# A gated mix of a state-space convolution and a GEGLU network: shared coefficient tables, a rotated contraction, products under the feed-forward matmuls, and one activation for GELU

## Chip, cores and metric

The kernel runs on one core of a Trainium2 chip. The metric is the device time of that core in microseconds (us), where lower is better. Each kernel was executed several times. Executions come in two states: in the slow one, TensorE's granted clock (the share of its full speed that the chip allowed, as the profile shows it) is lower over the whole run, and the time is longer. The span that a profile shows is the time from the first to the last instruction, and it is about 1.8 us shorter than the device time of the same execution.

## The reference

The output is `g*a + (1-g)*b` for an input of 2048 positions and 640 channels. `a` is a convolution with a generated filter, `b` is a feed-forward network, and `g` is a gate per position.

```python
# a: the filter of channel d at position l is a sum over N = 128 states
l = jnp.arange(L).astype(A_re.dtype)                # bfloat16
P = jnp.exp(logdA[:, :, None] * l[None, None, :])   # logdA = exp(log_dt) * (A_re + i A_im)
K = jnp.einsum("dn,dnl,dn->dl", Cc, P, dB).real     # 640 x 2048, dB = exp(log_dt) * B
# ... y = irfft(rfft(K, padded) * rfft(u, padded)), cut to L ...
a = y + u * Dskip
# b, with F = 1728
b = (gelu(x @ w_gate) * (x @ w_up)) @ w_down        # tanh form of GELU
g = sigmoid((x * gate_w).sum(-1, keepdims=True))    # x = u
```

One detail matters. The positions `l` are cast to bfloat16. They stay exact up to 256, then come in steps of 2 up to 512, of 4 up to 1024 and of 8 up to 2048. So `K` has only 257 + 3*128 = 641 different columns, not 2048.

## The kernel before

It works in strict stages. For each block of 64 channels it forms two tables, of 32 and 64 entries, so that their products give all 2048 positions. TensorE forms the phases, VectorE (DVE) reduces their range, and ScalarE (ACT) evaluates Exp, Abs and Sin. TensorE then contracts the tables over the 128 states:

```python
nc.scalar.activation(out=c1[:], in_=p1[:], func=ACT.Abs)
# ... c2; then Sin of c1, c2, p1, p2 (six ACT passes per block), four multiplications by the exponentials
nc.tensor.matmul(psK[:, ci, :], lhsT=c1[:, dl, :], rhs=c2[:, dl, :], start=True, stop=False)
nc.tensor.matmul(psK[:, ci, :], lhsT=p1[:, dl, :], rhs=p2[:, dl, :], start=False, stop=True)
```

After that come the forward transforms of filter and input (512 matmuls of 320 columns), the products of the two spectra on DVE, and the inverse transform (256 matmuls). Only then are the weights of the feed-forward network loaded. GELU is put together from a sigmoid:

```python
nc.scalar.copy(out=Gs[:fsz], in_=pGt[:fsz])
nc.scalar.copy(out=Us[:fsz], in_=pUt[:fsz])
nc.vector.tensor_tensor(out=q[:fsz], in0=Gs[:fsz], in1=Gs[:fsz], op=ALU.mult)
# ... two more DVE instructions on q ...
nc.scalar.activation(out=sg[:fsz], in_=q[:fsz], func=ACT.Sigmoid, scale=GELU_C)
nc.vector.tensor_tensor(out=sg[:fsz], in0=sg[:fsz], in1=Gs[:fsz], op=ALU.mult)
nc.vector.tensor_tensor(out=HT[:fsz, ft, toks], in0=sg[:fsz], in1=Us[:fsz], op=ALU.mult)
```

The down projection (448 matmuls) and the gated blend end the kernel.

## Time and profile before

The kernel had four executions, with a median of 777.4 us (775.29 to 991.85). The profiled one was the slow one:

```profile
core 0: 990.1 us, clock 0.569
```

The windows view cuts the span at the borders of the stages. The columns are the window, its length, the busy us of PE, PEld (weight loads), DVE, ACT and POOL (instruction counts in brackets), the granted clock, the share of DMA engine time, and GB/s.

```profile
0.00:370.00 370.00, 237.93 (x1690) 108.61 (x1691) 306.97 (x428) 289.26 (x229) 5.76 (x25) 0.61 0.09 18
391.00:505.00 114.00, 113.86 (x475) 62.53 (x475) 41.75 (x51) 41.26 (x61) 0.00 (x0) 0.56 0.00 1
505.00:622.00 117.00, 62.84 (x254) 33.67 (x252) 88.89 (x77) 0.26 (x1) 0.00 (x0) 0.53 0.00 0
622.00:642.00 20.00, 0.00 (x0) 0.00 (x0) 0.78 (x1) 0.00 (x0) 0.00 (x0) 0.51 0.97 243
642.00:861.00 219.00, 218.01 (x641) 76.92 (x642) 105.97 (x278) 95.89 (x170) 0.00 (x0) 0.55 0.06 21
861.00:990.10 129.10, 111.58 (x448) 46.58 (x446) 28.20 (x34) 12.16 (x18) 0.00 (x0) 0.55 0.06 21
```

The limit changes from stage to stage. Coefficients (to 370) are bound by DVE and ACT together, the transforms (to 505) by TensorE, the products (to 622) by DVE. From 622 to 642 TensorE does nothing while a weight load fills the DMA engines. The gate and up projection (to 861) is bound by TensorE, with DVE busy for half of it.

The groups view lists line of the kernel (L478 is line 478), engine, operation, tiles, shapes and count, then busy us and mean ns, then the idle time before them and what ended it.

```profile
L478 PE MATMUL pGt<-xT,Wg 128*128 128x512 bf16 (+1 forms) x280 | 118.5, 582 | 21.1 <-DMA Wg<-in_B_w_gate_dram 21.1
L283 PE MATMUL psK<-c,c 128*32 128x64 bf16 x640 | 68.2, 229 | 14.5 <-DVE c L272 9.3
L257 DVE TENSOR_SCALAR kM<-pph 128x512 f32<-128x512 f32 x120 | 80.6, 684 | 41.8 <-PE pph L248 26.9
```

The first line holds the 21 us weight gap. A "mean ns" of a matmul is its own latency, and matmuls overlap, so their cost is busy time divided by count (here 118.5 us / 280 = 423 ns, at a clock of 0.55).

### The profile page before, as it was taken

What the parts mean: (1) busy time and instruction counts of PE and PEld (TensorE: products, weight loads), DVE (VectorE), ACT (ScalarE), POOL (GpSimd) and SP (SyncE); (2) the same over time, 40 slices, a digit from 0 to 9 for tenths busy, and PEclk for the clock granted to TensorE, in tenths of its full rate; (3) what the DMA queues carried; (4) which work ended last, traced back from release to release, by engine and by line L of the source; (5) the groups of instructions that cost most, each with busy time, mean ns of one, the idle gap of its engine ahead of it and who ended that gap; (6) DMA issues with size and microseconds to landing.
All of it is one profiled execution on the core that took longest, in us unless ns stands there. A gap on an engine that the chain in (4) does not pass through costs nothing.

```text
span 990.1 us, 8897 instructions
## 1 busy us (share of the span) xinstructions
PE 755.7 (76%) x3556; PEld 333.8 (34%) x3556; DVE 585.5 (59%) x906; ACT 452.8 (46%) x492; POOL 6.3 (1%) x26
## 2 busy tenths in 40 slices
PE   0076787777797556999996605199999999988997
PEld 0022233323343253555553302033333333333333
DVE  6969878888888964045737897044544545422222
ACT  1259989899989956333310000044444444301000
POOL 2000000000000000000000000000000000000000
PEclk9975555555555555555555555555555555555555
DMA  2000000000000040000000000840000000000000
GB/s 53 0 0 1 1 12 11 11 1 12 12 12 11 1 129 11 0 1 1 1 1 0 1 0 0 222 153 1 0 1 0 1 0 1 0 21 21 20 27 21
DMA packets 44650, 19.01 MB, mean 19 GB/s; under 512 B 37248, under 2 KB 43328, under 8 KB 44608
## 3 DMA queue, kind: packets, MB, share of 16 engines
q1 hardware_dynamic: 44608, 18.44, 7.2%
q8 instruction: 28, 0.46, 0.2%
q14 instruction: 14, 0.11, 0.0%
HBM read 9.91 MB, written 2.62 MB: 13 GB/s over the span
## 4 chain that ended last, share of the span: by engine, by line
PE 66%; DVE 16%; ACT 14%; SPq 2%; DMA 1%; issue 1%; ACTq 0%; DVEq 0%
PE pU L372 11%; PE pD L502 11%; PE pGt L478 11%; PE pUt L481 11%; PE pY L408 6%; PE pa L252 2%; PE psK L283 2%; PE psK L284 2%; ACT c L267 2%; ACT p L269 2%; DVE kM L257 2%; DVE M L399 2%; DVE t L398 2%; DVE p L258 2%; ACT c L265 1%; DVE M L396 1%
## 5 line engine op out<-in xcount | busy, mean ns | idle before, releaser
L478 PE MATMUL pGt<-xT,Wg 128*128 128x512 bf16 (+1 forms) x280 | 118.5, 582 | 21.1 <-DMA Wg<-in_B_w_gate_dram 21.1
L502 PE MATMUL pD<-Wd,HT 128*128 128x512 bf16 (+1 forms) x448 | 111.8, 423 | 12.3 <-ACT b_sb L505 12.3
L484 ACT CAST Gs<-pGt 128x512 bf16<-128x512 f32 (+1 forms) x56 | 32.8, 586 | 191.4 <-PE pGt L478 191.4
L481 PE MATMUL pUt<-xT,Wu 128*128 128x512 bf16 (+1 forms) x280 | 118.3, 584 | 0.0
L257 DVE TENSOR_SCALAR kM<-pph 128x512 f32<-128x512 f32 x120 | 80.6, 684 | 41.8 <-PE pph L248 26.9
L408 PE MATMUL pY<-M,FI 128*128 128x320 bf16 x256 | 63.5, 443 | 54.1 <-DVE M L399 54.1
L253 PE MATMUL pph<-RX,b_bf 128*128 128x512 bf16 x80 | 40.8, 514 | 53.7 <-DVE p L258 52.7
L283 PE MATMUL psK<-c,c 128*32 128x64 bf16 x640 | 68.2, 229 | 14.5 <-DVE c L272 9.3
L283 PEld LDWEIGHTS <-c 128*32 128x32 bf16 x640 | 55.9, 116 | 66.1 <-DVE K L285 36.7
L258 DVE SCALAR_TENSOR_TENSOR p<-kM,pph 128x512 bf16<-128x512 f32 x120 | 77.8, 676 | 0.2
L488 DVE TENSOR_TENSOR q<-Gs 128x512 bf16<-128x512 bf16 (+1 forms) x56 | 23.8, 425 | 86.8 <-ACT Gs L484 86.8
L502 PEld LDWEIGHTS <-HT 128*128 128x128 bf16 x448 | 46.7, 123 | 78.0 <-issue 74.0
L284 PE MATMUL psK<-p,p 128*32 128x64 bf16 x640 | 67.9, 229 | 3.1 <-DVE p L273 3.1
L509 DVE TENSOR_TENSOR diff<-a_sb,b_sb 128x640 f32<-128x640 bf16 x16 | 13.2, 825 | 96.5 <-ACT b_sb L505 96.5
L372 PE MATMUL pU<-K_sb,FK 128*128 128x320 bf16 x256 | 62.7, 437 | 9.7 <-ACT FK L359 8.3
L478 PEld LDWEIGHTS <-Wg 128*128 128x128 bf16 (+1 forms) x280 | 37.0, 133 | 91.4 <-issue 91.4
L486 ACT CAST Us<-pUt 128x512 bf16<-128x512 f32 (+1 forms) x56 | 32.8, 586 | 66.3 <-PE pUt L481 49.2
L505 ACT CAST b_sb<-pD 128x640 bf16<-128x640 f32 x16 | 11.1, 692 | 112.5 <-PE pD L502 112.5
L408 PEld LDWEIGHTS <-FI 128*128 128x128 bf16 x256 | 34.1, 134 | 83.3 <-DVE M L399 50.5
L372 PE MATMUL pU<-a_sb,FU 128*128 128x320 bf16 x256 | 61.7, 438 | 0.0
L481 PEld LDWEIGHTS <-Wu 128*128 128x128 bf16 (+1 forms) x280 | 37.7, 135 | 69.9 <-issue 69.8
L284 PEld LDWEIGHTS <-p 128*32 128x32 bf16 x640 | 57.0, 118 | 6.2 <-issue 6.2
(140 smaller groups left out, 1120.8 us busy)
## 6 DMA issues: line engine op xcount, KB each, us to landing
K_sb<-K SPq DMA_DIRECT2D x40, 64.0 KB, 2.3
a_sb<-in_A_u_dram SPq DMA_DIRECT2D x4, 640.0 KB, 5.2
out_dram<-o_sb SPq DMA_DIRECT2D x16, 160.0 KB, 1.8
Wg<-in_B_w_gate_dram SPq DMA_DIRECT2D x1, 2160.0 KB, 8.5
Wu<-in_B_w_up_dram SPq DMA_DIRECT2D x1, 2160.0 KB, 13.3
Wd<-in_B_w_down_dram SPq DMA_DIRECT2D x1, 2080.0 KB, 19.2
dsk<-in_A_Dskip_dram SPq DMA_DIRECT2D x1, 160.0 KB, 3.4
Are<-in_A_A_re_dram SPq DMA_DIRECT2D x1, 160.0 KB, 3.5
```

The lines of the kernel that those rows point to most:

```text
L253: nc.tensor.matmul(pph[:], lhsT=lhs_b, rhs=rhs_rx, start=True, stop=True)
L257: nc.vector.tensor_scalar(out=kM[:], in0=tau_src, scalar1=MAGIC, scalar2=None, op0=ALU.add)
L258: nc.vector.scalar_tensor_tensor(out=pt[:, :, xs], in0=kM[:], scalar=-MAGIC, in1=tau_src, op0=ALU.add, op1=ALU.subtract)
L283: nc.tensor.matmul(psK[:, ci, :], lhsT=c1[:, dl, :], rhs=c2[:, dl, :], start=True, stop=False)
L284: nc.tensor.matmul(psK[:, ci, :], lhsT=p1[:, dl, :], rhs=p2[:, dl, :], start=False, stop=True)
L372: nc.tensor.matmul(pU[:, h, 0:DH], lhsT=tab[:, k, q, f0:min(512, f0 + 256):2], rhs=src[:, 4 * b + k, h * DH:(h + 1) * DH], start=(k == 0), ...
L408: nc.tensor.matmul(pY[:, h, 0:DH], lhsT=FI[:, ft, q, 128 * mo:128 * mo + 128], rhs=M[:, q, ft, h * DH:(h + 1) * DH], start=(q == 0 and ft ...
L478: nc.tensor.matmul(pGt[:fsz, :], lhsT=Wg[:, kt, f0:f0 + fsz], rhs=xT[:, kt, toks], start=(kt == 0), stop=(kt == nkt - 1))
L481: nc.tensor.matmul(pUt[:fsz, :], lhsT=Wu[:, kt, f0:f0 + fsz], rhs=xT[:, kt, toks], start=(kt == 0), stop=(kt == nkt - 1))
L484: nc.scalar.copy(out=Gs[:fsz], in_=pGt[:fsz])
L486: nc.scalar.copy(out=Us[:fsz], in_=pUt[:fsz])
L502: nc.tensor.matmul(pD[:, d0:d0 + dn], lhsT=HT[:fsz, ft, toks], rhs=Wd[:fsz, ft, d0:d0 + dn], start=(ft == 0), stop=(ft == nft - 1))
```

## The change

The intent is to do less coefficient work, and to let stages that use different engines run at the same time. The kernel is largely rewritten, with all tiles at fixed places in one memory area, which the profile calls `arena`. Cut to its core and regrouped by purpose:

```diff
 # 1. Coefficients at 32 x 21 = 672 positions, four chunks of 160 channels; the second table holds these bases:
+X2 = [0, 1, 2, 3, 4, 5, 6, 7, 256, 258, 260, 262, 512, 516, 768, 772, 1024, 1280, 1536, 1792, 2048]
 # ... exponentials: one activation per table entry, its step given as the scale; phases are 16-bit
 # fixed-point numbers that wrap by themselves, so Abs and DVE's range reduction go ...
-            nc.scalar.activation(out=c1[:], in_=p1[:], func=ACT.Abs)
-                    nc.tensor.matmul(psK[:, ci, :], lhsT=c1[:, dl, :], rhs=c2[:, dl, :], start=True, stop=False)
-                    nc.tensor.matmul(psK[:, ci, :], lhsT=p1[:, dl, :], rhs=p2[:, dl, :], start=False, stop=True)
+            for g in range(gh):
+                for q in range(2):
+                    for j in range(4):
+                        d = G4 * j + gh * hb + g
+                        nc.tensor.matmul(psK[hb][32 * j:32 * j + 32, NX2 * g:NX2 * g + NX2], lhsT=cs1[:, q, :, d],
+                                         rhs=cs2[:, q, :, d], start=(q == 0), stop=(q == 1))
 # ... the transform table of the filter sums the positions that round to one value ("selection") ...
 # 2. The input's transform runs inside the coefficient stage:
+        phases(k)
+        last_sin[0] = sines(k)
+        u_some(2)
+        scaled(k)
 # 3. Filter transform and products go by frequency tile, and are free to run under the feed-forward matmuls:
+    for ft in range(NF):
+        kb, gt = k_fwd(ft)
+        Mf.append(products(ft, kb, gt))
 # 4. GELU is one activation:
-                nc.scalar.activation(out=sg[:fsz], in_=q[:fsz], func=ACT.Sigmoid, scale=GELU_C)
+                gi = nc.scalar.activation(out=Gs[:], in_=pG[:], func=ACT.Gelu_apprx_tanh)
 # 5. The inverse transform joins the down projection, both at 320 columns, and the gate goes into the last additions:
+                    nc.tensor.matmul(pD[:, 0:DH], lhsT=HT[c][0:fz, ft, ts], rhs=Wd[0:fz, ft, hs],
+                                     start=(ft == 0), stop=(ft == NFT - 1))
 # ...
+                        nc.tensor.matmul(pY[:, 0:DH], lhsT=tab[:, ft, q, ts], rhs=Mf[ft][:, q, c, hs],
+                                         start=(q == 0 and ft == 0), stop=(q == 1 and ft == NF - 1))
 # ... many lines cut ...
```

In the contraction, both operands now step through memory by 160 elements, which is 320 bytes.

## The prediction

> **What bounds the kernel now.** The profiled execution is a slow one: 990 us, mean granted TensorE clock 0.569, against 775 to 778 us for three others. By busy time per stretch: coefficient generation, 0 to 370 us (ACT busy 289, DVE 307); forward transforms to 505 (PE 114 of 114); products and inverse to 622 (DVE 89, PE waits 54 for DVE); 20 us without PE work (waits: 21.1 for the Wg load); gate and up projection to 861 (PE 218 of 219); down projection to the end. The groups show ACT spending 167 us in Abs and Sin and about 55 in table loads.
>
> Here a 512-column matmul starts every 382 ns, a 320-column one every 0.22 us (timeline). The Trainium skill ("TensorE: Matmul & The Clock Gate", Back-to-back issue gap) gives N/2.4 + 2.5 ns warm: 216 and 136 ns. With those (estimate) the PE-bound stages lose about 195 of the 214 us between slow and fast runs, so I take fast runs to be near full clock. No trace here shows one.
>
> **What changes.** The coefficients are evaluated at 672 points instead of 2048, over tables of 32 + 21 entries instead of 32 + 64; +/- pairs share sines. ACT (estimates: 0.83 ns per element, from traced lengths, plus 0.1 to 0.2 us each): 106 Exp 40, 20 Sin 42, tables 8, 32 spectrum copies 20, table loads 10. Total 120 us in place of 290. DVE here: phases and scaling about 22 us per 160-column chunk, four chunks, plus weights, selection tables and copies: 140 in place of 307; DVE becomes the pacer. The input transform (256 matmuls) hides here. The kernel transform falls from 256 to 144 matmuls; coefficient selection adds 44.
>
> GELU becomes one activation: five DVE instructions per FFN tile become one (112 to about 20 us). Products keep their elements but split by frequency: about 114 us of DVE, now under the FFN's 138 us of PE. The inverse (256 matmuls) merges with the down projection (448), all at 320 columns: 704 x 136 ns = 96 us.
>
> **New risk.** The contraction keeps 1280 small matmuls, but reads both operands with a 320-byte stride. Before they were contiguous, about 29 ns apiece. The skill ("SBUF — State Buffer", Door 1: The DMA port swizzle) says each access crossing to a new 16-byte line pays a penalty; no run here shows its size. I take 50 ns: 64 us. The second table has one buffer and DVE's PSUM copies queue in order, so I count most of this as exposed.
>
> **Sum, fast state.** First sine at 53; DVE's 20 groups, second exponentials and exposed contraction about 155, so FFN starts near 207; FFN with products 155 (PE 138; DVE 134, starting late); last stage with its weight load 100; tail 5. About 465 us.
>
> Predicted 465 us, 80% range 410 to 535. Faster by over 2%: 0.98; within: 0.01; slower: 0.01. A slow run would be about 600.
>
> **What shows it right.** Groups: contraction spacing 30 to 100 ns; DVE about 140 us before the FFN; Sin about 42 us. Waits: ACT or DVE on the contraction. Stages: FFN near 155 us with PE busy 85% or more; last stage with PE always busy; the weight gap gone.
>
> **What would make it wrong.** Contraction at 100 ns or more (+65 us) or without penalty (-25); small DVE instructions costing more than 0.25 us start to start; DVE trailing PE at the FFN's end, delaying the inverse; denser PE work being granted a lower clock.

## Result and profile after

The changed kernel took 450.95 us (median of 8 executions, 449.02 to 452.74). By then the kernel before had 13 executions with a median of 777.03 us; only the first one, at 991.85, was slow; no run here explains why. The ratio is 0.5804, with a 95% interval of 0.5794 to 0.5814. Ratios here are the mean time of one kernel's fast runs over that of the other's fast runs of the same rounds, so they are not quite the ratio of the medians quoted. The result is correct.

The profiled execution is a fast one. The cores view, and the windows view with the same columns as before:

```profile
core 0: 448.3 us, clock 0.931
```

```profile
0.00:52.30 52.30, 5.00 (x16) 1.90 (x17) 30.22 (x63) 36.58 (x72) 0.95 (x7) 1.00 0.22 50
52.30:90.00 37.70, 26.45 (x425) 17.79 (x425) 32.37 (x80) 24.45 (x22) 1.74 (x12) 0.86 0.08 22
90.00:130.00 40.00, 29.13 (x432) 16.47 (x431) 32.17 (x64) 35.61 (x68) 0.00 (x0) 0.87 0.18 42
130.00:168.00 38.00, 20.03 (x395) 13.61 (x394) 32.21 (x72) 19.86 (x17) 0.00 (x0) 0.79 0.23 62
168.00:193.50 25.50, 7.74 (x345) 5.99 (x344) 9.25 (x22) 6.02 (x4) 0.00 (x0) 0.57 0.96 215
193.50:345.60 152.10, 146.34 (x758) 69.35 (x759) 138.08 (x194) 84.13 (x141) 0.00 (x0) 0.99 0.13 33
345.60:445.00 99.40, 99.17 (x679) 63.57 (x678) 45.39 (x76) 0.00 (x0) 0.00 (x0) 1.00 0.13 43
```

The coefficient stage, with the whole input transform in it, ends at 193.5 instead of near 390. Over the three middle windows DVE is the busiest engine (96.8 of 115.7 us, against 79.9 for ACT and 75.6 for TensorE). It does not pace the stage alone: from 90 to 130, where the second exponentials run, ACT is busier (35.6 of 40 us), and DVE itself waits 15.0 us for the contraction. From 193.5 to 345.6, TensorE (146 of 152 us) and DVE (138) are both nearly full. That is the overlap at which the change aims. In the last 99.4 us TensorE is always busy.

The groups that answer to those shown of before:

```profile
L490 PE MATMUL pG<-arena 128*128 128x512 bf16 x260 | 67.7, 386 | 1.5 <-DVE arena L505 1.4
L369 PE MATMUL psK<-arena 128*32 128x21 bf16 x1280 | 20.7, 213 | 26.0 <-DVE arena L356 15.5
L339 ACT ACTIVATE arena<-arena 128x2240 bf16<-128x2240 int16 (+1 forms) x20 | 43.4, 2177 | 22.9 <-DVE arena L332 20.6
```

The gate matmuls no longer wait for their own weights. The 1280 small matmuls of the contraction are busy for 20.7 us in all, 16 ns apiece. The sines, with their cosines, take 43.4 us.

The seam between the two halves is not clean. The timeline of TensorE and of SP (SyncE, the engine that issues most transfers) from 178 us on shows start, length, engine, line, what, how many, and in square brackets the idle time before and its releaser:

```profile
178.12 3.66 PE L369 MATMUL psK<-arena 128*32 128x21 bf16 x237 [15.51 <-DVE arena L356]
...
182.94 0.53 SPq L456 DMA_DIRECT2D arena<-in_B_w_up_dram  x1
183.51 5.83 SPq L470 DMA_TRANSPOSE arena<-in_A_u_dram  x2
...
186.04 1.41 PE L369 MATMUL psK<-arena 128*32 128x21 bf16 x83 [4.25 <-issue]
...
189.44 11.82 SPq L376 DMA_DIRECT2D arena<-arena  x16
...
193.53 2.32 PE L493 MATMUL pU<-arena 128*128 128x512 bf16 x5 [3.41 <-DMA arena<-in_B_w_up_dram]
```

TensorE waits 15.5 us for DVE to scale the last tables, pauses for 4.25 us within the contraction (see the run with another loop order below), and waits 3.4 us for the up weights. The 16 small copies that spread the filter's values over partitions (L376) are issued one after another, 0.74 us each, and only from 189.4 on. The first product needs them, and starts at 204.8. From there to 340.9 DVE is busy for 132 of 136 us and TensorE for 133 (windows view). That the late start of the products sets the end of this stage is read from several traces: in seven of them (this one and six of the experiments below) the last product starts 136.3 to 138.2 us after the first filter spectrum is out, whenever that is. This is its end:

```profile
340.42 0.48 DVE L441 TENSOR_TENSOR arena<-arena 128x640 bf16<-128x640 bf16 x1
...
340.93 0.37 SPq L517 DMA_DIRECT2D arena<-in_B_w_down_dram  x1
...
345.61 2.11 PE L536 MATMUL pD<-arena 128*128 128x320 bf16 x12 [1.47 <-DMA arena<-in_B_w_down_dram]
```

The rest of the down weights goes where the products had their buffers. So its load starts only after the last product, and the last stage with it.

### The profile page after: what moved, and what is told of

Its sections match the earlier page's. It is cut to its first block, busy times and chain, and to the rows that moved or that the text cites. A ratio compares the mean times of both kernels' runs of the same rounds, so it can differ in the third digit from the quotient of the medians.

```text
span 448.3 us, 7434 instructions
## 1 busy us (share of the span) xinstructions
PE 333.9 (74%) x3046; PEld 188.7 (42%) x3046; DVE 320.1 (71%) x568; ACT 206.6 (46%) x321; POOL 2.7 (1%) x19
## 4 chain that ended last, share of the span: by engine, by line
PE 43%; DVE 31%; ACT 12%; DMA 6%; SPq 5%; issue 2%; DVEq 0%; ACTq 0%
PE pD L536 14%; PE pY L543 8%; DVE arena L441 5%; PE pT L413 5%; DVE arena L440 4%; PE pT L204 4%; DVE arena L438 3%; PE psK L369 3%; PE pU L493 3%; PE pG L490 3%; DVE arena L498 3%; DVE arena L437 3%; ACT arena L339 3%; SPq L470 2%; SPq L376 2%; DMA arena<-in_B_w_up_dram 2%
## 5 line engine op out<-in xcount | busy, mean ns | idle before, releaser
L204 PE MATMUL pT<-arena 128*128 128x320 bf16 x256 | 51.0, 366 | 72.3 <-ACT arena L174 43.9
L536 PE MATMUL pD<-arena 128*128 128x320 bf16 x448 | 69.7, 300 | 1.5 <-DMA arena<-in_B_w_down_dram 1.5
L493 PE MATMUL pU<-arena 128*128 128x512 bf16 x260 | 67.6, 384 | 3.4 <-DMA arena<-in_B_w_up_dram 3.4
L490 PE MATMUL pG<-arena 128*128 128x512 bf16 x260 | 67.7, 386 | 1.5 <-DVE arena L505 1.4
L204 PEld LDWEIGHTS <-arena 128*128 128x128 bf16 x256 | 29.3, 117 | 93.0 <-ACT arena L174 45.6
L536 PEld LDWEIGHTS <-arena 128*128 128x128 bf16 x448 | 43.6, 97 | 26.1 <-issue 10.1
L339 ACT ACTIVATE arena<-arena 128x2240 bf16<-128x2240 int16 (+1 forms) x20 | 43.4, 2177 | 22.9 <-DVE arena L332 20.6
L495 ACT ACTIVATE arena<-pG 128x512 bf16<-128x512 f32 x52 | 31.1, 598 | 39.9 <-PE pG L490 38.3
L496 ACT CAST arena<-pU 128x512 bf16<-128x512 f32 x52 | 30.5, 587 | 27.1 <-PE pU L493 27.0
L543 PE MATMUL pY<-arena 128*128 128x320 bf16 x256 | 40.5, 300 | 2.2 <-DVE arena L505 2.2
L538 DVE SCALAR_TENSOR_TENSOR arena<-pD,omg,arena 128x320 f32<-128x320 f32 x32 | 17.6, 550 | 34.0 <-PE pD L536 34.0
L369 PE MATMUL psK<-arena 128*32 128x21 bf16 x1280 | 20.7, 213 | 26.0 <-DVE arena L356 15.5
L493 PEld LDWEIGHTS <-arena 128*128 128x128 bf16 x260 | 25.0, 98 | 33.0 <-DMA arena<-in_B_w_up_dram 4.2
L490 PEld LDWEIGHTS <-arena 128*128 128x128 bf16 x260 | 25.4, 99 | 31.9 <-issue 4.4
L440 DVE TENSOR_TENSOR arena<-arena 128x2560 bf16<-128x2560 bf16 (+3 forms) x32 | 31.4, 982 | 2.5 <-ACT arena L415 2.5
L545 DVE SCALAR_TENSOR_TENSOR arena<-pY,g_f,arena 128x320 bf16<-128x320 f32 x32 | 17.6, 552 | 19.8 <-PE pY L543 19.8
L441 DVE TENSOR_TENSOR arena<-arena 128x2560 bf16<-128x2560 bf16 (+3 forms) x32 | 31.4, 982 | 0.0
L543 PEld LDWEIGHTS <-arena 128*128 128x128 bf16 x256 | 22.5, 98 | 14.4 <-issue 2.4
## 6 DMA issues: line engine op xcount, KB each, us to landing
arena<-in_B_w_up_dram SPq DMA_DIRECT2D x1, 2160.0 KB, 10.5
```

Source lines behind the costliest of these rows:

```text
L204: nc.tensor.matmul(pU[:, h, 0:DH], lhsT=tab[:, k, q, fsl(ft)], rhs=ublk[b][:, k, h * DH:(h + 1) * DH], start=(k == 0), stop=(k == 3))
L339: return nc.scalar.activation(out=dst, in_=ph_tile(k)[:].bitcast(I16)[:, :, 0:n, 0:2 * CH:2], func=ACT.Sin, scale=SIN_SCALE)
L369: nc.tensor.matmul(psK[hb][32 * j:32 * j + 32, NX2 * g:NX2 * g + NX2], lhsT=cs1[:, q, :, d], rhs=cs2[:, q, :, d], start=(q == 0), stop=(q ...
L440: nc.vector.tensor_tensor(out=t1[:, 0:nb, :], in0=U[:, 1, 0:nb, :], in1=g[k1], op=ALU.mult)
L441: nc.vector.tensor_tensor(out=dst, in0=dst, in1=t1[:, 0:nb, :], op=op1)
L490: nc.tensor.matmul(pG[:], lhsT=Wg[:, kt, f0:f0 + 128], rhs=xT[:, kt, :], start=(kt == 0), stop=(kt == NKT - 1))
```

## Experiments

Twelve kernels were run. The runs of the kernel before had medians of 777.14, 776.18 and 775.81 us. The changed kernel itself was timed apart from these, so a difference from it is also a difference of two ratios.

My theory was this. The gain has two sources of about equal rank: less coefficient work on ACT and DVE, and DVE's products moved under TensorE's feed-forward work, which only fits because the new GELU frees DVE. The rivals were: the slow profile had misled me about fast runs; the new GELU is worth something by itself; the contraction's cost is off the critical path; and the memory stride makes the contraction slow, or else the rotation over column groups makes it fast.

### The kernel before, once more, for a fast profile

There is no edit.

> The kernel before, unchanged, to get a profile of its fast state, which no trace so far shows. Theory of the prediction (fast means near full clock, so that the PE-bound stages shrink and the coefficient stage hardly does): 777 us, granted clock above 0.85; gate and up projection 120 to 130 us, last stage 70 to 80, forward transforms 68 to 75, coefficient stage 335 to 360. Rival (fast runs are throttled less, but still throttled): clock 0.7 to 0.8, gate and up projection 145 to 165 us, and the coefficient stage below 320.

It took 775.31 us at a clock of 0.854. Its time is that of the fast ones. Its windows, cut at its own stage borders:

```profile
0.00:359.00 359.00, 189.30 (x1700) 89.65 (x1700) 309.51 (x445) 288.74 (x230) 6.32 (x26) 0.81 0.09 19
359.00:437.00 78.00, 73.21 (x511) 50.52 (x512) 45.51 (x68) 54.74 (x75) 0.00 (x0) 0.95 0.00 1
437.00:537.00 100.00, 42.19 (x259) 27.07 (x257) 93.01 (x83) 0.69 (x1) 0.00 (x0) 0.71 0.00 0
537.00:558.00 21.00, 0.00 (x0) 0.00 (x0) 0.55 (x1) 0.00 (x0) 0.00 (x0) 0.60 1.02 269
558.00:687.50 129.50, 126.79 (x640) 57.44 (x640) 99.65 (x270) 89.23 (x167) 0.00 (x0) 0.99 0.08 29
687.50:769.00 81.50, 68.45 (x449) 34.78 (x448) 29.40 (x41) 13.24 (x21) 0.00 (x0) 1.00 0.09 31
```

The stages that TensorE bounds shrink from 219 to 129.5 us (gate and up) and from 129 to 81.5 us (down). The coefficient stage, bound by DVE and ACT, goes only from 370 to 359. This is what the prediction had worked out from the slow profile. Its size was somewhat too large: the transforms, the gate and up projection and the last stage lost 36, 89.5 and 43 us, 169 in all, where the estimate for the stages bound by TensorE was about 195.

It also gives the account of the gain, with spans. Before, coefficients and input transform took 359 + 35 = 394 us (the 256 input matmuls are one stretch of 34.9 us in this trace) and the rest 379.5 us. After, these are 193.5 and 254.8 us. So about 200 us come from the coefficient side and about 125 us from everything behind it. No run takes back one of the coefficient edits alone, so how the 200 us divide is not shown. Candidates are the fewer table entries per channel (53 instead of 96), the range reduction that DVE no longer does (L257 and its partner L258 filled 158 us of the slow profile), the Abs passes, and the input transform that now runs alongside.

### GELU as one activation, in the kernel before

```diff
-                nc.scalar.copy(out=Gs[:fsz], in_=pGt[:fsz])
+                nc.scalar.activation(out=Gs[:fsz], in_=pGt[:fsz], func=ACT.Gelu_apprx_tanh)
 # ... the chain of q and sg is gone ...
-                nc.vector.tensor_tensor(out=HT[:fsz, ft, toks], in0=sg[:fsz], in1=Us[:fsz], op=ALU.mult)
+                nc.vector.tensor_tensor(out=HT[:fsz, ft, toks], in0=Gs[:fsz], in1=Us[:fsz], op=ALU.mult)
```

> One part of the change alone: the kernel before with the GELU as a single activation, four DVE instructions and a sigmoid per tile fewer. Theory: in the kernel before the gate and up projection is bound by PE (2.16 us of matmuls per tile against about 1.65 us of DVE), so removing 80 to 90 us of DVE work buys nothing: 765 to 780 us, within 2%. Rival: in the fast state DVE and ACT pace that stage: 740 to 755 us.

It took 771.67 us (770.89 to 772.41), a ratio of 0.9928 (0.9913 to 0.9943). Its window of the gate and up stage:

```profile
557.60:683.20 125.60, 125.42 (x641) 57.52 (x641) 23.37 (x55) 69.17 (x116) 0.00 (x0) 0.98 0.09 32
```

DVE's work in the gate and up stage fell from 99.7 to 23.4 us, yet the stage only went from 129.5 to 125.6 us, with TensorE busy for 125.4. Here DVE was not what the stage waited for.

### The sigmoid chain put back into the changed kernel

```diff
-                gi = nc.scalar.activation(out=Gs[:], in_=pG[:], func=ACT.Gelu_apprx_tanh)
+                nc.scalar.copy(out=Gs[:], in_=pG[:])
-                    nc.vector.tensor_tensor(out=ht[:, ft, :], in0=Gs[:], in1=Us[:], op=ALU.mult)
+                    gelu_chain(ht[:, ft, :], Gs[:])
+                    nc.vector.tensor_tensor(out=ht[:, ft, :], in0=ht[:, ft, :], in1=Us[:], op=ALU.mult)
```

> The same part undone in the changed kernel: the sigmoid chain back, everything else as changed. Theory: there the DVE shares the stage with the products (138 us busy of 152), so the chain's four extra instructions per tile, about 1.25 us x 56 = 70 us, land on the critical path: stage 210 to 225 us instead of 152, total 505 to 530 us. Rival (PE still bounds the stage, as in the kernel before): 451 to 460 us.

It took 521.51 us, a ratio of 0.6716 (0.6701 to 0.6731), 70.6 us more than the change. The feed-forward window of this run:

```profile
194.40:418.00 223.60, 152.99 (x749) 69.82 (x750) 206.24 (x405) 112.61 (x197) 0.00 (x0) 0.83 0.09 23
```

DVE is now busy for 206 of 223.6 us and TensorE for 153. So the same edit is worth 5.5 us in one kernel and 70.6 us in the other, because there DVE shares the stage with the products. One wait of 41 us, in which TensorE stood behind a small DVE copy (see below), is in this run too, and the run was not repeated with that copy at high priority. So part of the 70.6 us may be the order of the queue. DVE's work alone bounds that part: it fills 206 us, 54 more than the whole stage took in the change.

### The products kept in front of the feed-forward stage

A copy of one element from the last product into the place of the gate weights, ahead of their load, makes that load wait for all products.

```diff
+    nc.vector.tensor_copy(out=Wg[:, 0, 0:1], in_=Mf[NF - 1][:, 0, 0, 0:1])
     nc.sync.dma_start(out=Wg[:], in_=B_w_gate.rearrange("(k p) f -> p k f", p=128))
```

> The overlap of spectrum products and FFN taken away: the gate weights' load waits for the last product, nothing else changes. Theory (the products' 114 us of DVE hide behind the FFN's matmuls): stage about 255 us (products 114 to 130, then a load of 10, then the FFN at 115 to 120) instead of 152, total 540 to 565 us. Rival (the gain comes from cheaper parts and not from running them side by side): total below 480 us.

It took 549.40 us, a ratio of 0.7061 (0.7045 to 0.7077), 98.5 us more than the change. The waits view (waiter, releaser, us in total, times, longest):

```profile
PE pG L491 <- DMA arena<-in_B_w_gate_dram: 49.2, 1, 49.2
```

The edit also leaves the gate weights' load uncovered, which took 8.4 us from issue to landing. The overlap is thus worth about 90 us of the gain, 98 with that load. This number and the one before must not be added, as both measure how well the same stage is filled.

### The column group as the outermost loop of the contraction

```diff
-            for g in range(gh):
-                for q in range(2):
-                    for j in range(4):
+            for j in range(4):
+                for g in range(gh):
+                    for q in range(2):
```

> Asks why the contraction with strided operands took 16 ns of busy time per matmul where the prediction had 50 and the contiguous one of the kernel before about 29. Same 1280 matmuls, same operands, same results; only the loop order: all matmuls of one 32-column group after each other instead of the four groups in turn. Theory A (the four groups overlap, and that alone hides the cost of the strided reads): 50 ns or more each, contraction 64 us or more over the run, total up by 15 to 40 us. Theory B (a 320-byte stride costs nothing here): about 29 ns each as in the kernel before, total up by 3 to 12 us. Theory C (neither matters): 16 ns, same time. The pauses in the contraction marked issue should shrink as the matmuls get slower, if they are instruction supply.

It took 485.76 us, a ratio of 0.6251 (0.6234 to 0.6267), 34.8 us more than the change. These are the contraction of the second chunk in this run, and of the first chunk in the changed kernel:

```profile
112.09 17.40 PE L369 MATMUL psK<-arena 128*32 128x21 bf16 x320 [0.26 <-DVE arena L356]
```

```profile
74.85 2.18 PE L369 MATMUL psK<-arena 128*32 128x21 bf16 x136
78.02 2.07 PE L369 MATMUL psK<-arena 128*32 128x21 bf16 x128 [0.99 <-issue]
81.47 1.02 PE L369 MATMUL psK<-arena 128*32 128x21 bf16 x56 [1.39 <-issue]
```

With one column group at a time a matmul takes 17.40 / 320 us = 54 ns, and the stream has no pauses. With four groups in rotation it takes 2.18 / 136 us = 16 ns, but the stream stops for 1.0 to 1.4 us between bursts.

These stops, marked "issue", are waits for instructions, by all that the traces show. The four contractions of the changed kernel have six of them, 10.5 us in all with the 4.25 us of the seam. Counted in the packed trace, they lie 256, 768, 768, 256 and 512 instructions of TensorE's queue apart, to within one. The DMA view has a queue, q8, of the kind "instruction". Its packets hold 16,384 bytes, and their number goes with TensorE's instructions at 256 apiece: 24 packets for 6106 instructions here, 19 for 4826 in the second run below with half of the contraction. Each stop ends 1.2 to 1.4 us after such a packet has landed. Within the stop of 4.25 us, while weights and transposes filled the DMA engines, it was this one:

```profile
q8 instruction: 1, 0.02, 1.8%
```

The slow loop uses up its instructions more slowly, and has no such stop.

The windows of the slow loop show the same rate at two clocks:

```profile
112.10:116.00 3.90, 3.90 (x71) 3.90 (x72) 1.83 (x8) 3.87 (x9) 0.00 (x0) 1.00 0.01 2
118.00:129.00 11.00, 11.00 (x210) 11.00 (x208) 0.60 (x1) 11.00 (x32) 0.00 (x0) 0.50 0.01 3
```

The rates are 18 and 19 matmuls per us at clocks of 1.00 and 0.50. So the array's clock does not set them, and the supply of operands may. The rotation hides most of that cost. My 50 ns, a guess, came close for a single column group and was three times too high for this kernel. From first to last matmul the four contractions take 31.2 us in the change and 69.7 us here. Of these 38.5 us, 34.8 appear in the time, so nearly all of it is exposed (no other work covers it). How much of the 54 ns is due to the stride was not isolated. In the kernel before, contiguous operands and 64 columns gave about 29 ns in bursts at full clock, and 53 ns at half clock. Those matmuls also went to one column group, in accumulating pairs; so the stride is the likely cause of the 54 ns, but no run changed it alone.

### Half of the contraction

Only the cosine part is computed. The result is wrong, though within the tolerance of the comparison.

```diff
-                for q in range(2):
+                for q in range(1):
 # ... start and stop of the one matmul left are both True ...
```

> Half of the contraction's matmuls taken away (cosine products only; the result is wrong on purpose). The prediction counted most of the contraction's time as exposed. Theory from the trace (only the last chunk and short DVE waits for the PSUM copies are exposed, and the last chunk hides behind the weight load): total down by 0 to 6 us. Rival (exposed as predicted): down by 12 us or more.

It took 480.28 us, a ratio of 0.6182 (0.6167 to 0.6197). With less work it was 29 us slower, so both expectations missed. The waits view tells why:

```profile
PE pG L490 <- DVE g_l L479: 44.1, 1, 44.1
```

The scheduler, which orders each engine's instructions, had put a copy of four gate values (0.16 us of work) behind a series of products in DVE's queue. TensorE needed the buffer from which this copy reads, and stood for 44 us. As a measure of the contraction this run is worthless. It was repeated with that copy at high priority:

```diff
-                for q in range(2):
+                for q in range(1):
 # ... as before; and in the feed-forward part: ...
-        nc.vector.tensor_copy(out=g_l[:, 4 * tq:4 * tq + 4], in_=pL[:, 0:4])
+        with tc.high_priority():
+            nc.vector.tensor_copy(out=g_l[:, 4 * tq:4 * tq + 4], in_=pL[:, 0:4])
```

> Half of the contraction's matmuls taken away again (wrong result on purpose), after the first try came out 29 us slower because PE waited 44 us for a 4-column copy of gate logits that stood behind products in DVE's queue. Now that copy has high priority, so that the queue's order no longer spoils the comparison. Theory (the contraction is exposed almost one to one, as the run with one column group at a time suggests: 39 us more of it cost 35): about 15 us of contraction less, total 434 to 441 us. Rival (hidden except at the end): 446 to 451.

It took 436.89 us (433.48 to 438.65), a ratio of 0.5619 (0.5594 to 0.5645), 14 us less than the change. Its four contractions take 13.6 us from first to last matmul, 17.6 less than in the change, because half the matmuls also have fewer and shorter stops. So about four fifths of the contraction is exposed, against nine tenths with one column group at a time. The waits view shows where: DVE's copies out of the contraction wait for it. In the change, with one column group at a time, and with half of the matmuls:

```profile
DVE arena L371 <- PE psK L369: 15.0, 6, 6.2
DVE arena L371 <- PE psK L369: 53.4, 8, 9.0
DVE arena L371 <- PE psK L369: 3.0, 4, 1.4
```

This wait grows by 38.4 us where the time grows by 34.8, and shrinks by 12.0 where the time falls by 14. The high priority alone was not run.

### Weight loads from ACT's queue

The up weights' load stood behind transposes in SP's queue. Here both weight loads are issued from ACT's queue, the first of them earlier (the tiles' definitions move up with them).

```diff
+        if k == 17:
+            nc.scalar.dma_start(out=Wg[:], in_=B_w_gate.rearrange("(k p) f -> p k f", p=128))
 # ... and after the loop
+    nc.scalar.dma_start(out=Wu[:], in_=B_w_up.rearrange("(k p) f -> p k f", p=128))
 # ... the two loads on nc.sync are gone ...
```

> The two FFN weight loads issued from the ACT queue inside the coefficient loop, instead of behind the small coefficient copies and input transposes on the SP queue; same bytes, same buffers. Theory (PE's wait at the FFN's start, 168 to 193.5 us, ends with the up-projection weights, issued at 182.9 although their buffer was free at 178.1): FFN starts 4 to 7 us earlier, total 444 to 447 us. Rival (the DMA engines, at 0.96 busy there, set the landing): within 2 us of 451.

It took 448.78 us (447.21 to 452.70), a ratio of 0.5785 (0.5755 to 0.5815). That is 2 us less than the change, less than I expected, and its interval overlaps with the change's: a gain is not shown. The first up matmul came 4.4 us earlier (189.1), but the small copies still ran to about 199. The first filter spectrum came only 2.7 us earlier (201.4 for 204.1), and the last product 2.6 us earlier.

The next run split both weights in column halves (1024 and 640 columns), so that two of the four loads could start even earlier:

```diff
+        if k == 17:
+            w_load(Wg1, B_w_gate, 0, F1)
+            w_load(Wu1, B_w_up, 0, F1)
 # ... after the loop the other halves, Wg2 and Wu2; the matmuls pick the half ...
```

> As the run before, and both weight matrices split by columns, so that the first 1024 columns of each lie where the first exponential table was, which is free after group 16; only the last 640 wait for group 19. Theory: the FFN starts when the contraction of the last chunk ends, at 183 to 187 us, 7 to 11 us earlier than in the changed kernel; total 440 to 444 us. Rival (DMA bandwidth sets it): no better than the run before.

It took 455.37 us, a ratio of 0.5857 (0.5839 to 0.5875), and was 1% slower than the change, against the expectation. The timeline of ACT, and the contraction that follows:

```profile
176.67 0.39 ACTq L392 DMA_DIRECT2D arena<-in_B_w_up_dram  x1
177.10 2.07 ACT L339 ACTIVATE arena<-arena 128x2240 bf16<-128x2240 int16 x1 [12.00 <-DMA arena<-in_A_u_dram]
...
187.70 2.50 PE L369 MATMUL psK<-arena 128*32 128x21 bf16 x157 [23.97 <-DVE arena L356]
```

A load that must wait before it is issued holds back everything behind it on the same queue. ACT, with sines to compute, stood for 12 us. The last contraction started at 187.7 instead of 178.1. The profile names a transpose of the input as what the load waited for; I did not find out why it depended on that.

### The start

In the changed kernel ACT waits 9.5 us at the start for a chain of weights on DVE, which itself waits for ACT's exponentials. The edit computes the weights between the two groups of exponentials, and their arctangent behind them.

```diff
     def exps(pair, nu=0):
 # ... the 32 exponentials of the first table
+        if pair == 0:
+            weights()
 # ... the 21 of the second; at the top level, in place of weights():
+    weights_end()
```

> The changed kernel with the weight phases computed between the two halves of the first exponentials, so that DVE's reciprocal and products run while ACT works on the second half; two table loads more. Theory (the first Sin at 52.3 us waits for a chain ACT-DVE-ACT after all 53 exponentials, and from there DVE paces the groups): first Sin at 44 to 46 us, total 442 to 445. Rival (DVE's total work paces the stage from the start, so an earlier start is lost again): within 2 us of 451.

It took 441.86 us (440.39 to 444.05), a ratio of 0.5691 (0.5672 to 0.5710), 9 us less than the change. ACT's timeline in the changed kernel and then in this one, from the arctangent to the first sine:

```profile
39.93 0.74 ACT L274 ACTIVATE arena<-arena 128x640 f32<-128x640 f32 x1 [9.49 <-DVE arena L273]
...
52.30 2.34 ACT L339 ACTIVATE arena<-arena 128x2560 bf16<-128x2560 int16 x1 [2.30 <-DVE arena L332]
```

```profile
31.86 0.74 ACT L278 ACTIVATE arena<-arena 128x640 f32<-128x640 f32 x1
...
44.25 2.34 ACT L344 ACTIVATE arena<-arena 128x2560 bf16<-128x2560 int16 x1 [2.30 <-DVE arena L337]
```

The first sine comes 8.1 us earlier. The median falls by 9 us; between these two traces the span falls by 6.0 us (448.3 to 442.3), the profiled execution being the slowest of its four. So most of the start is exposed, perhaps all of it.

### Two combinations

The first one joins the new start, the weight loads from ACT's queue, and the high priority of the small copy.

```diff
+            weights()
 # ... weights_end() as above; in the coefficient loop and after it: ...
+            nc.scalar.dma_start(out=Wg[:], in_=B_w_gate.rearrange("(k p) f -> p k f", p=128))
+    nc.scalar.dma_start(out=Wu[:], in_=B_w_up.rearrange("(k p) f -> p k f", p=128))
 # ... and around the copy of the gate values:
+        with tc.high_priority():
```

> The changed kernel with the earlier start, the FFN weight loads on the ACT queue, and the gate logit copy at high priority. If the two gains add: 438 to 443 us against 451. If the end of the FFN stage is set by the products, which start when the coefficient copies on the SP queue have landed, the second gain mostly vanishes: 441 to 444.

It took 443.93 us (440.03 to 445.31), a ratio of 0.5696 (0.5673 to 0.5719), no better than the start alone. The parts don't add up. The first filter spectrum comes at 196.7 us, against 198.1 with the new start alone, but the last product starts at 334.9, against 334.4.

The second one also sends half of the last chunk's small copies through ACT's queue, and issues the up weights before the last contraction (cut here).

```diff
-                nc.sync.dma_start(out=Kt[32 * q:32 * q + 32, 0:na, CH * ch + G4 * j:CH * ch + G4 * j + G4],
+                eng = nc.scalar if ch == NCH - 1 and j >= 2 else nc.sync
+                eng.dma_start(out=Kt[32 * q:32 * q + 32, 0:na, CH * ch + G4 * j:CH * ch + G4 * j + G4],
```

> As best_a, and half of the last chunk's sixteen small coefficient copies (0.74 us of issue each on SP, 12 us together) issued from the ACT queue. Theory (the products wait for those copies): kernel transform and products start 4 to 6 us earlier, total 3 to 5 us below best_a. Rival (ACT's late PSUM copies for the FFN cost as much): within 1 us of best_a, or slower.

It took 440.89 us (440.41 to 441.69), a ratio of 0.5677 (0.5664 to 0.5690). The 16 copies were issued in 6.1 us, not 11.8; the first filter spectrum came at 191.3 and the last product started at 329.2, against 204.1 and 340.4 in the change. This is the fastest median of a kernel that computes everything. It beats the kernel before and, by about 2.2% (0.5677 / 0.5804 = 0.978), the change. It is not clearly faster than the new start alone, whose interval overlaps with its own.

## Why the prediction was right

The time was predicted as 465 us (410 to 535) and measured as 450.95. Point by point:

- **Fast runs are near full clock: right.** A fast run of the kernel before had a clock of 0.99 in the gate and up stage, and took 129.5 us where the slow one took 219. The rate that I took from the Trainium skill ("TensorE: Matmul & The Clock Gate", Back-to-back issue gap), N/2.4 + 2.5 ns, holds in the trace of the changed kernel: five matmuls of 512 columns take 1.08 us, which is 216 ns each.
- **The coefficient side: right in size.** ACT was busy for 122.5 us before 193.5 us (predicted 120), with 43.4 for sines (42). DVE was busy for 136 us (140). The first sine came at 52.3 (53). DVE is the busiest engine of the loop, as said, but ACT and the contraction hold it up in places, so it is not the only pacer.
- **GELU and the products: right.** The stage took 152.1 us (155), TensorE being busy for 96% of it. The two GELU experiments show the reason: 5.5 us without the products in the stage, 70.6 us with them. Keeping the products in front costs 98.5 us.
- **The last stage: right.** It took 99.4 us (100), with TensorE always busy.
- **The contraction: mis-sized.** I took 50 ns per matmul and 64 us. The runs showed 16 ns and 20.7 us busy, or 31.2 us with the stops for instructions, which I had not counted at all. The term was about 33 us too high. I had costed the stride and left out the rotation over four column groups; a single group measured 54 ns. That the term is exposed was right: half of it was worth 14 us.
- **The weight gap gone: wrong.** From 168 to 193.5 us TensorE was busy for only 7.7 of 25.5 us. The wait for weights proper shrank from 21 to 3.4 us. In its place stand the wait for DVE's last scaling and a pause of 4.25 us in the contraction. This offset part of the error above: the feed-forward matmuls started in earnest at 193.5, not 207, which is 13.5 us early instead of 33.

So the sum came within about 3% partly by luck, because a term that was too large met losses that I had not counted.

## What to carry to other kernels

Look at the data before the schedule: rounding in the inputs left 641 of 2048 coefficient columns, and the larger part of the gain (about 200 us) lies on the coefficient side, though no run shows how much of it the rounding alone gives. What an edit is worth depends on which engine its stage waits for: the same GELU edit gave 5.5 us in one kernel and 70.6 us in the other, so work should be taken off an engine together with the plan for what fills it. Where small matmuls read strided operands, rotate them over TensorE's column groups (54 ns became 16 here), and expect so dense a stream to run into the supply of instructions (10.5 us here); and look in every in-order queue for a small item that stands behind large ones, as a 0.16 us copy cost 44 us here and a waiting load held ACT for 12 us.

## What the Trainium skill lacked or had wrong

- "TensorE: Matmul & The Clock Gate", "Wait — 56ns, not 53.3ns?" says that start-to-start "never drops below ≈25 ns however small N is". With four column groups in rotation and 21 columns, 136 matmuls started in 2.18 us, which is 16 ns each. The floor is not one for matmuls in different column groups; the page's own part on packing small matmuls has such matmuls run "concurrently in the same array", but the floor is stated without that exception.
- The same page, "Back-to-back issue gap", gives a sustained 131 ns per matmul at 512 columns and calls 216 ns the isolated figure. In this kernel the sustained stream ran at 216 ns (five in 1.08 us), and the 704 matmuls of 320 columns at 141 ns (99.4 us in all), close to the page's formula.
- "SBUF — State Buffer", "Door 1: The DMA port swizzle" says that crossing to a new 16-byte line costs a penalty, but no size. With operands 320 bytes apart and one column group, a matmul of 21 columns cost 54 ns, at granted clocks of 1.00 and of 0.50 alike. In rotation over four groups it was 16 ns. As no run changed the stride alone, this bounds the penalty and does not measure it.
- "Runtime: NRT & Kernel Launch", "Instruction fetch mechanics" calls refills of 256 instructions "mostly hidden". In the dense contraction, where a matmul with its weight load takes 16 ns, they were not: its six stops lie whole multiples of 256 instructions apart, to within one, and each ends 1.2 to 1.4 us after a 16,384-byte packet of instructions has landed. They cost 1.0 to 1.4 us each, and 4.25 us while the DMA engines were full. At 54 ns per matmul there was no stop.
- "ScalarE: Activation LUTs", "What ACT_TABLE_LOAD costs" gives 1283 ns for the load, which this trace shows too (1.28 us), and a drain of 1380 ns more for every switch. Here the next activation started right after the load: in the changed kernel an activation ended at 26.28, the load ran from 26.30 to 27.58, and the next one started at 27.59.
- "DMA: Bandwidth & Descriptors", "Issuing engines are not separate DMA queues" says that issuing from a second engine only saves issue time, usually small beside the transfer itself. For small copies it was not negligible: 0.74 us of issue against 1.9 us from issue to landing, so that 16 of them took 11.8 us to issue from one queue and 6.1 us from two. That section doesn't say that a load which waits on ACT's queue stops ACT's computing (12 us here).
